# An RWKV scan feeding a SoLU layer: three weight pieces loaded ahead of the second chunk, and one split moved behind the exponential

## The chip, the core and the metric

The kernel runs on one core of a Trainium2 chip. The metric is the device time of one execution in microseconds, median of three runs: 345.81 us (345.55 to 346.35) for the kernel before. The profile is of one execution of its own and counts from the first to the last instruction: 343.4 us.

## The reference

Two parts stand one behind the other. The first is a linear recurrence over time (RWKV) for 4 batches, 8 heads, 768 steps and a head size of 48; its output is read as a matrix `x` of 3072 rows and 384 columns. The second is a SoLU layer on `x`:

```python
for t in range(S):
    cur = einsum('bhd,bhe->bhde', u * kt, vt)
    y[:, :, t] = einsum('bhd,bhde->bhe', rt, state + cur)
    state = w[..., None] * state + einsum('bhd,bhe->bhde', kt, vt)
h = x @ w_in                                # 384 -> 1024
sm = softmax(h);  solu = h * sm
ln = (solu - mean) / sqrt(var + 1e-6) * g_ln
return ln @ w_out                           # 1024 -> 384
```

The weights `w_in` and `w_out` arrive as 64-bit floats, and the kernel turns them into 32-bit floats itself, as integers.

## The kernel before

**Tiling.** The 3072 rows are 24 chunks of 128 rows (6 time steps of the tiling by 4 batches, the batch running fastest, so chunks 0 to 3 are the four batches' first rows). Every chunk goes through two stages: attention, which makes its `xT` (the chunk's `x`, turned), and the layer, which makes its output rows. The layer of a chunk trails its attention.

**Order of the work.** Nothing is planned by a scheduler: under `manual_schedule` every engine executes its instructions in the order in which the Python code issues them, and waits on semaphores for what the other engines have to deliver. So moving one call moves its instructions in the queues of all engines that it uses, and what stands behind a waiting instruction on its engine waits too.

**Steps of a chunk's attention in the prologue** (L1031 to L1105, chunks 0 to 4), by the names that the text uses:

- `load(i, "kr")`, `load(i, "v")` (L472): rows of k, r and v, each 192 KB, issued on SyncE's queue (SP).
- `decay_k(i)` (L697): GpSimd (POOL) multiplies k by a table of decays, tile `kp`.
- `weigh(i)` (L710, L711): POOL makes `rku` = k u r in two multiplications. `sum_own(i)` (L715): VectorE (DVE) sums it per head into `own`. `diagonal(i)` (L729): ScalarE (ACT) writes eight diagonal matrices from `own` into `AT`, the score matrix of the chunk.
- `turn_r(i)` (L741, L742): TensorE (PE) transposes r, DVE multiplies it out of PSUM. `turn_k(i)` (L749, L751): PE transposes `kp`, ACT copies it out.
- `whole_scores(i)` (L764): PE multiplies k and r into the two score banks. `take_scores(i)` (L788): DVE copies them under a mask over `AT`, two instructions. 
- `whole_y(i)` (L815): PE multiplies `AT` and v. `take_y(i)` (L864): ACT copies the result out as `xT`. `whole_outer(i)` (L889) and `update(i)` (L910 to L916): the new state.

**Weights.** `w_in` is cut into six pieces of 512 KB (0 to 5: pieces 0, 1, 2 are the three row blocks of its first 512 columns, 3, 4, 5 those of the other 512), `w_out` into eight of 384 KB (6 to 13). A piece is loaded by `load_weights` (L511) and converted in three steps on three engines: `convert_a` (L522, ACT, the low words), `convert_b` (L535, L537, DVE, the high words), `convert_c` (L545, POOL, their sum). `take_up(p)` is `convert_a(p)` and the load of the next piece that is not yet loaded.

**The layer.** `ffn_in(j)` (L926, L931): six matmuls, three for each half of 512 columns (`ffn_in(0, (0,))` and `(0, (1,))` in the prologue do one half each), then ACT's exponential `e`. There is one `h_ps` buffer, so the next `ffn_in` waits until `unit(j)` has read it: DVE's reciprocal and product (L937, L939), then two passes on ACT (L941, L942). `halve_ln(j)` (L977, ACT) splits the chunk's result into 16-bit halves in a buffer `halves`, from which a transposing DMA (L966) makes another; `join_ln(j)` (L971, DVE) joins them to `lnT`; `ffn_out(j)` (L1016, PE) multiplies with `w_out`. `halve_rk` and `join_rk` do the same for r and k of later chunks. The `halves` buffers and the raw weight pieces are one pool of six.

**Fillers.** `spin(n)` (L593) is n matmuls of the identity into the `h_ps` buffer, of no use but to keep TensorE busy.

**The steady loop** (L1180 to L1260) takes two chunks, a pair, at a time: attention of chunks i and i + 1, `ffn_in` and `unit` of j = i - 2 and j + 1, `ffn_out` of l = i - 7 and l + 1. Its first turn is i = 7, the second pair is i = 9. On ACT the second pair's queue begins, in the kernel before:

```python
if l + 2 < N:
    halve_ln(l + 2)        # ACT: 16-bit halves, needs a free `halves` buffer
for n in first:
    diagonal(n)            # ACT: 8 instructions
join_ln(l + 1)             # DVE
...
if j < N and not late:
    ffn_in(j)              # PE, then ACT: exponential
    unit(j)                # DVE, ACT
```

Of the kernel before, what the change touches and what calls it, by code (L numbers as in the profile page):

```python
# [399 lines left out]
def direct_path(  # L400
# [29 lines left out]
    nc = tc.nc  # L430
# [10 lines left out]
    LA, LO, FIRST, WHOLE = 2, 5, 9, 7  # L441
# [26 lines left out]
    def load(i, which="krv"):  # L468
        b, c = units[i]
        for t, src, n in ((kpads, k, "k"), (rpads, r, "r"), (vts, v, "v")):  # L470
            if n in which:
                nc.sync.dma_start(out=t[i % len(t)][:, :, 0:D],  # L472
                                  in_=src[b, :, ts(c, T), :].rearrange("h s d -> s h d"))
# [34 lines left out]
    def load_weights(j, tag="raw", bufs=6):  # L508
        dst, src, _ = pieces[j]
        raws[j] = wpool.tile([128, dst.shape[1], 2], U32, tag=tag, name="raw", bufs=bufs)  # L510
        nc.sync.dma_start(out=raws[j].rearrange("p n o -> p (n o)"), in_=src)  # L511
# [13 lines left out]
    def convert_b(j):  # L525
        hi, low = step[j]
        n = low.shape[1]
        ma = wpool.tile([128, n], U32, tag="ma", name="ma", bufs=4)
        part = ma
        if pieces[j][2] is None:  # L530
            part = psM.tile([128, n], F32, tag="m", name="part").bitcast(U32)

        nc.vector.tensor_scalar(out=part, in0=hi, scalar1=3, scalar2=0x3FFFFFF8,  # L535
                                op0=ALU.logical_shift_left, op1=ALU.bitwise_and)
        nc.vector.scalar_tensor_tensor(out=ma, in0=hi, scalar=0xC0000000, in1=part,  # L537
                                       op0=ALU.bitwise_and, op1=ALU.bitwise_or)
        step[j] = ma, low

    def convert_c(j):
        dst, _, f = pieces[j]
        ma, low = step[j]

        nc.gpsimd.tensor_tensor(out=dst.bitcast(U32) if f is None else ma, in0=ma, in1=low,  # L545
                                op=ALU.add)
# [19 lines left out]


    load(0, "kr")
    load_weights(0)
    load(1, "kr")  # L570
    load(0, "v")
    load_weights(1)
    load(2, "kr")
    load_weights(2)
    load(1, "v")
    load_weights(3)
    load_weights(4)
    load_weights(5)
    load(3, "kr")
    load(2, "v")  # L580
# [8 lines left out]
    def spin(n):  # L589

        ps = psH.tile([128, dff], F32, tag="h", name="spin")
        for _ in range(n):
            nc.tensor.matmul(ps[:, 0:128], ident, ident, start=True, stop=True)  # L593
# [67 lines left out]
    N = len(units)  # L661
# [32 lines left out]
    def decay_k(i):  # L694
        X = live.setdefault(i, {})
        X["kp"] = apool.tile([128, H, P], F32, name="kp", bufs=5)
        nc.gpsimd.tensor_mul(X["kp"].rearrange("p h d -> p (h d)"),  # L697
                             kpads[i % NLD].rearrange("p h d -> p (h d)"),
                             kdec.rearrange("p a d -> p (a d)"))
# [8 lines left out]
    def weigh(i, engine):  # L708
        rku = live[i]["rku"] = apool.tile([128, H, D], F32, name="rku")
        engine.tensor_mul(rku, kpads[i % NLD][:, :, 0:D], u_bc)  # L710
        engine.tensor_mul(rku, rku, rpads[i % NLD][:, :, 0:D])  # L711

    def sum_own(i):
        own = live[i]["own"] = small.tile([128, H, 1], F32, name="own")
        nc.vector.tensor_reduce(out=own[:, :, 0], in_=live[i]["rku"], axis=AX.X, op=ALU.add)  # L715
# [21 lines left out]
    def turn_r(i):  # L737
        rT = factors(i)["rT"]
        ps = psM.tile([128, HP, T], F32, tag="m", name="tr_ps")
        for a in range(HP):  # L740
            nc.tensor.transpose(ps[:, a, :], pair(rpads[i % NLD], a), ident)  # L741
        nc.vector.tensor_mul(rT, ps, fore)  # L742

    def turn_k(i):
        X = live[i]
        ps = psM.tile([128, HP, T], F32, tag="m", name="tk_ps")

        for a in range(HP):
            nc.tensor.transpose(ps[:, a, :], pair(X["kp"] if i > 0 else kpads[0], a), ident)  # L749
        if i > 0:  # L750
            nc.scalar.copy(out=X["kT"], in_=ps)  # L751
        else:
            nc.vector.tensor_mul(X["kT"], ps, back)
# [30 lines left out]
    def take_scores(i):  # L784
        A4 = live[i]["AT"].rearrange("p (a q) t -> p a q t", q=2)
        mask = later if i < WHOLE else later_half
        for q in range(2):
            nc.vector.copy_predicated(A4[:, :, q, :], mask.to_broadcast([128, HP, mask.shape[2]]),  # L788
                                      live[i]["scores"][q])
# [69 lines left out]
    def take_y(i):  # L859
        X = live[i]  # L860
        X["xT"] = fpool.tile([128, KD, 128], F32, name="xT", bufs=LA + 1)
        n = T // len(X["y"])
        for c, y in enumerate(X["y"]):
            nc.scalar.copy(out=X["xT"][:, :, ts(c, n)], in_=y)  # L864
# [159 lines left out]
    def take_up(p):  # L1024
        nonlocal ahead
        convert_a(p)
        if ahead < len(pieces):
            load_weights(ahead)
            ahead += 1
# [9 lines left out]
    spin(2)  # L1039
    whole_scores(0)  # L1040
    convert_b(0)
    decay_k(1)
    weigh(1, nc.gpsimd)
    turn_r(1)
    spin(4)
    turn_k(1)
    take_scores(0)
    convert_c(0)
    sum_own(1)
    take_up(1)  # L1050
    diagonal(1)
    spin(3)
    whole_y(0)
    whole_outer(0)
    convert_b(1)
    convert_c(1)
    whole_scores(1)
    update(0)
    take_y(0)
    decay_k(2)  # L1060
    weigh(2, nc.gpsimd)
    turn_r(2)
    take_up(2)
    spin(4)
    turn_k(2)
    take_scores(1)
    convert_b(2)
    convert_c(2)
    load(5, "kr")
    load(3, "v")  # L1070
    whole_y(1)
    whole_outer(1)
    whole_scores(2)
    take_up(3)
    take_y(1)
    convert_b(3)
    convert_c(3)
    sum_own(2)
    ffn_in(0, (0,))
    take_up(4)  # L1080
    convert_b(4)
    convert_c(4)
    load(6, "kr")
    load(4, "v")
    take_up(5)
    diagonal(2)
    convert_b(5)
    convert_c(5)
    ffn_in(0, (1,))
    update(1)  # L1090
    take_scores(2)
# [88 lines left out]
    for i in range(LA + LO, N + LA + LO, 2):  # L1180
        j, l = i - LA, i - LA - LO

        late = i == LA + LO
        for n in (i + 5,) if late else (i + 6, i + 7):
            if n < N:
                load(n, "kr")
        for n in (i + 3, i + 4) if not late else ():
            if n < N:
                load(n, "v")
        first, second = ([n] if n < N else [] for n in (i + 2, i + 3))  # L1190
        if late:
            decay(i + 3)
            diagonal(i + 1)
            halve_k(i + 3)
            ffn_in(j)
            attend([i, i + 1])
            halve_r(i + 3)
            unit(j)
            sum_own(i + 3)
            load(i + 3, "v")  # L1200
            load(i + 4, "v")
        decay(i + 4)
        for n in (j - 2, j - 1):
            if LO - 1 <= n < N:
                deviation(n)
        decay(i + 5)
        if l + 2 == N:
            check_sums()
        if l + 2 < N:
            halve_ln(l + 2)  # L1210
        for n in first:
            diagonal(n)
        join_ln(l + 1)
        for n in first:
            join_rk(n)
        if j < N and not late:
            ffn_in(j)
            unit(j)
            within([i, i + 1])
        if i + 4 < N and not late:  # L1220
            halve_rk(i + 4)
        check_next()
        ffn_out(l)
        if late:
            load(i + 6, "kr")
            within([i, i + 1])
            ffn_in(j + 1)
            halve_rk(i + 4)
            load(i + 7, "kr")
        for n in (i, i + 1):  # L1230
            if n < N:
                carried(n)
        if l + 3 < N:
            halve_ln(l + 3)
        for n in (i, i + 1):
            if n < N:
                take_y(n)
        for n in (i, i + 1):
            if n < N:
                update(n)  # L1240
        if late:
            unit(j + 1)
        for n in second:
            join_rk(n)
        if j + 1 < N and not late:
            ffn_in(j + 1)
        for n in second:
            diagonal(n)
        if j + 1 < N and not late:
            unit(j + 1)  # L1250
        ffn_out(l + 1)
        halve_rk(i + 5)
        for n in (i + 4, i + 5):
            if n < N:
                sum_own(n)
        attend([i + 2, i + 3])
        if l + 2 < N:
            join_ln(l + 2)
        if i >= N - 7:
            check_next()  # L1260
# [43 lines left out]
```

## Time and profile before

| | |
|---|---|
| time, median (lowest to highest) | 345.81 us (345.55 to 346.35) |
| span in the profile, granted TensorE clock | 343.4 us, 0.996 |
| `h_ps` matmuls (L926), `o_ps` matmuls (L1016) | 129.9 us, 128.3 us busy |
| ACT copies to `halves` (L977) | 45.3 us busy, 10.2 us idle before them, waiting for a DMA |
| DMA | 52.69 MB, mean 153 GB/s |

The page gives the busy time of each engine, the chain of work that ended last, and groups of instructions with the idle time of their engine just before them. A line of a timeline reads: start, length (us), engine, source line, operation, tiles, number of instructions merged, and in brackets the idle time before the first of them and what ended it. A line of a table of waits reads: who waited for whom, us in total, times, the longest. The chain that ended last is 73% TensorE. From 112 us to the end TensorE's timeline has no gap; the gaps, and the fillers, lie before that.

### The profile page before, as it was taken

How to read it: one execution, taken by the hardware profiler on the slowest of the kernel's cores; microseconds unless marked ns; L12 is line 12 of the kernel's file. 1: busy time of each engine (PE TensorE's matmuls, PEld its weight loads, DVE VectorE, ACT ScalarE, POOL GpSimd, SP SyncE). 2: the span in 40 equal slices, each digit the busy share in tenths (PEclk: the TensorE clock that was granted, in tenths of full speed). 3: DMA queues.
4: the chain of work that ended last, by engine and by line, in shares of the span. 5: the costliest groups of instructions: out<-in, count | busy, mean ns of one | idle time of the engine just before them, and what ended most of it. 6: DMA issues, size and time to landing. Idle time of an engine off the chain costs nothing.

```text
span 343.4 us, 10629 instructions
## 1 busy us (share of the span) xinstructions
PE 332.8 (97%) x4483; PEld 198.9 (58%) x4483; DVE 210.6 (61%) x379; ACT 234.4 (68%) x477; POOL 174.4 (51%) x202
## 2 busy tenths in 40 slices
PE   8989999999998999999999999999999999999993
PEld 6856566655565556556556556555555555555563
DVE  8796988889766487576576577575365052332410
ACT  4776887997945968885784794796594466456510
POOL 7798987699997387682683683630300000000000
PEclk9999999999999999999999999999999999999998
DMA  7999998389999999989969969859841432454541
GB/s 149 243 252 215 253 210 135 68 107 196 208 154 191 174 224 177 205 145 171 198 132 177 212 105 155 186 112 153 191 105 38 122 101 63 99 130 111 131 99 40
DMA packets 164742, 52.69 MB, mean 153 GB/s; under 512 B 157901, under 2 KB 161102, under 8 KB 164686
## 3 DMA queue, kind: packets, MB, share of 16 engines
q1 hardware_dynamic: 164684, 51.92, 80.8%
q8 instruction: 37, 0.61, 0.8%
q14 instruction: 19, 0.16, 0.2%
q10 hardware_dynamic: 2, 0.00, 0.0%
HBM read 26.75 MB, written 4.72 MB: 92 GB/s over the span
## 4 chain that ended last, share of the span: by engine, by line
PE 73%; POOL 11%; ACT 4%; DVE 4%; issue 3%; DMA 2%; SPq 0%; ACTq 0%; POOLq 0%; DVEq 0%
PE o_ps L1016 32%; PE h_ps L926 30%; PE at L854 3%; POOL kp L697 3%; PE at L843 3%; POOL rku L711 2%; POOL rku L710 2%; PE at L781 2%; DMA halves<-halves 2%; POOL rp L704 2%; PE kv_ps L880 1%; ACT AT L729 1%; PE y_ps L815 1%; POOL state L914 1%; DVE ma L537 1%
## 5 line engine op out<-in xcount | busy, mean ns | idle before, releaser
L926 PE MATMUL h_ps<-w_in_sb,xT 128*128 128x512 f32 x288 | 129.9, 600 | 2.0 <-DVE solu L939 2.0
L1016 PE MATMUL o_ps<-w_out_sb,lnT 128*128 128x384 f32 (+1 forms) x400 | 128.3, 476 | 0.0
L1016 PEld LDWEIGHTS o_ps<-w_out_sb,lnT 128*128 128x128 f32 x400 | 74.3, 190 | 48.9 <-issue 4.3
L926 PEld LDWEIGHTS h_ps<-w_in_sb,xT 128*128 128x128 f32 x288 | 52.7, 190 | 61.9 <-issue 57.0
L931 ACT ACTIVATE e<-h_ps 128x1024 f32<-128x1024 f32 x24 | 24.6, 1024 | 40.7 <-PE h_ps L926 40.7
L977 ACT COPY halves<-solu 128x2048 uint16<-128x2048 uint16 x24 | 45.3, 1889 | 10.2 <-DMA halves<-halves 10.2
L914 POOL TENSOR_TENSOR state<-state,pw 48x192 f32<-48x192 f32 x32 | 23.1, 722 | 49.1 <-DVE state L910 47.1
L971 DVE COPY lnT<-halves 128x2048 uint16<-128x2048 uint16 x24 | 39.5, 1660 | 10.7 <-DMA halves<-halves 10.4
L941 ACT ACTIVATE solu<-solu,st 128x1024 f32<-128x1024 f32 x24 | 27.5, 1146 | 24.7 <-DVE solu L939 24.7
L948 POOL TENSOR_SCALAR st<-st 128x1 f32<-128x1 f32 x24 | 4.7, 195 | 64.2 <-ACT e L942 64.1
L710 POOL TENSOR_TENSOR rku<-kpad,u_bc 128x384 f32<-128x384 f32 x24 | 31.9, 1329 | 9.7 <-DVE own L715 8.9
L729 ACT ACTIVATE AT<-same,own 128x64 f32<-128x64 f32 x136 | 34.2, 338 | 0.0
L697 POOL TENSOR_TENSOR kp<-kpad,kdec 128x512 f32<-128x512 f32 x24 | 30.6, 1275 | 3.6 <-ACT kdec L646 1.6
L711 POOL TENSOR_TENSOR rku<-rku,rpad 128x384 f32<-128x384 f32 x24 | 31.3, 1303 | 1.9
L939 DVE SCALAR_TENSOR_TENSOR solu<-h_ps,st,e 128x1024 f32<-128x1024 f32 x24 | 30.8, 1284 | 2.0
L565 DVE TENSOR_REDUCE least<-mag 128x1 f32<-128x384 f32 (+1 forms) x14 | 8.5, 607 | 35.3 <-ACT mag L563 35.3
L937 DVE RECIPROCAL st<-sums 128x1 f32<-128x1 f32 x24 | 3.8, 160 | 40.5 <-ACT e L931 40.0
L1018 ACT ACTIVATE o<-o_ps,st 128x384 f32<-128x384 f32 (+1 forms) x25 | 13.9, 558 | 18.6 <-PE o_ps L1016 12.6
L942 ACT ACTIVATE e<-solu 128x1024 f32<-128x1024 f32 x24 | 25.4, 1057 | 0.8
L971 DVE COPY rk<-halves 128x2048 uint16<-128x2048 uint16 x15 | 25.2, 1679 | 0.2
L788 DVE COPY_PREDICATED AT<-later_half,at 128x256 f32<-128x256 uint32 x34 | 12.5, 438 | 16.1 <-PE at L781 15.7
L704 POOL TENSOR_TENSOR rp<-rpad,rdec 128x512 f32<-128x512 f32 x15 | 21.2, 1414 | 0.0
(105 smaller groups left out, 388.6 us busy)
## 6 DMA issues: line engine op xcount, KB each, us to landing
raw<-in_moe_w_in_dram SPq DMA_DIRECT2D x12, 512.0 KB, 5.2
raw<-in_moe_w_out_dram SPq DMA_DIRECT2D x16, 384.0 KB, 3.8
kpad<-in_k_dram SPq DMA_DIRECT2D x24, 192.0 KB, 4.9
rpad<-in_r_dram SPq DMA_DIRECT2D x24, 192.0 KB, 5.0
vt<-in_v_dram SPq DMA_DIRECT2D x24, 192.0 KB, 5.5
out_dram<-o SPq DMA_DIRECT2D x23, 192.0 KB, 3.4
halves<-halves SPq DMA_TRANSPOSE x39, 5.3
out_dram<-o SPq DMA_DIRECT2D x2, 96.0 KB, 2.7
```

The costliest lines, as they stand in the source:

```text
L697: nc.gpsimd.tensor_mul(X["kp"].rearrange("p h d -> p (h d)"), kpads[i % NLD].rearrange("p h d -> p (h d)"), kdec.rearrange("p a d -> p (a ...
L704: nc.gpsimd.tensor_mul(X["rp"].rearrange("p h d -> p (h d)"), rpads[i % NLD].rearrange("p h d -> p (h d)"), rdec.rearrange("p a d -> p (a ...
L710: engine.tensor_mul(rku, kpads[i % NLD][:, :, 0:D], u_bc)
L711: engine.tensor_mul(rku, rku, rpads[i % NLD][:, :, 0:D])
L729: nc.scalar.activation(out=AT[:, h, :], in_=unit_matrix, func=ACT.Copy, scale=X["own"][:, h])
L914: nc.gpsimd.tensor_mul(S, S, wT)
L926: nc.tensor.matmul(h_ps[:, ts(n, NX)], X["xT"][:, j, :], w_in_sb[:, j, ts(n, NX)], start=(j == 0), stop=(j == KD - 1))
L939: nc.vector.scalar_tensor_tensor(out=solu, in0=X["h"], scalar=rs, in1=X["e"], op0=ALU.mult, op1=ALU.mult, accum_out=tot)
L941: nc.scalar.activation(out=solu, in_=solu, func=ACT.Identity, scale=-float(dff), bias=tot)
L971: nc.vector.tensor_copy(out=words.bitcast(U16).rearrange("p n (t o) -> p o n t", o=2), in_=turned)
L977: nc.scalar.copy(out=both.rearrange("p (o n) -> p o n", o=2), in_=split(X["solu"]))
L1016: nc.tensor.matmul(o_ps, X["lnT"][:, f, :], w_out_sb[:, f, part], start=(f == 0), stop=(f == KF - 1))
```

## The change

It has two parts, and no instruction is added or taken out but four fillers.

The first is a new order of the prologue. In the loads, v of chunk 0 and the pieces 0, 1 and 2 of `w_in` now stand ahead of k and r of chunk 1. The calls behind it are reordered to suit: the conversions of pieces 0 and 1 come before chunk 1's attention, pieces 2 and 3 in the midst of it, `weigh(2)` behind the conversion of piece 4, the first half of `ffn_in(0)` ahead of chunk 2's transposes, and one `spin(4)` (in the kernel before between `turn_r(2)` and `turn_k(2)`) is gone. It is meant to have the first matmuls of the layer ready for TensorE earlier.

The second concerns the second pair alone: `halve_ln(l + 2)` is issued behind `ffn_in(j)` and `unit(j)` instead of ahead of `diagonal`, so that on ACT the exponential no longer stands behind a copy that waits for its buffer.

```diff
     load(0, "kr")
+    load(0, "v")
     load_weights(0)
+    load_weights(1)
+    load_weights(2)
     load(1, "kr")
-    load(0, "v")
-    load_weights(1)
+    load_weights(3)
+    load(1, "v")
+    load_weights(4)
     load(2, "kr")
-    load_weights(2)
-    load(1, "v")
-    load_weights(3)
-    load_weights(4)
     load_weights(5)
...
     whole_scores(0)
     convert_b(0)
+    convert_c(0)
+    take_up(1)
+    convert_b(1)
     decay_k(1)
+    spin(4)
+    take_scores(0)
+    turn_r(1)
+    spin(3)
+    turn_k(1)
     weigh(1, nc.gpsimd)
-    turn_r(1)
-    spin(4)
-    turn_k(1)
-    take_scores(0)
-    convert_c(0)
-    sum_own(1)
-    take_up(1)
-    diagonal(1)
-    spin(3)
     whole_y(0)
     whole_outer(0)
-    convert_b(1)
+    take_up(2)
+    take_y(0)
     convert_c(1)
-    whole_scores(1)
-    update(0)
-    take_y(0)
-    decay_k(2)
-    weigh(2, nc.gpsimd)
-    turn_r(2)
-    take_up(2)
-    spin(4)
-    turn_k(2)
-    take_scores(1)
     convert_b(2)
     convert_c(2)
+    whole_scores(1)
+    sum_own(1)
+    diagonal(1)
+    update(0)
+    take_up(3)
+    convert_b(3)
+    convert_c(3)
+    ffn_in(0, (0,))
+    decay_k(2)
+    turn_r(2)
     load(5, "kr")
     load(3, "v")
+    take_up(4)
+    convert_b(4)
+    take_scores(1)
+    turn_k(2)
+    convert_c(4)
     whole_y(1)
     whole_outer(1)
+    take_y(1)
+    weigh(2, nc.gpsimd)
+    take_up(5)
+    convert_b(5)
+    convert_c(5)
     whole_scores(2)
-    take_up(3)
-    take_y(1)
-    convert_b(3)
-    convert_c(3)
     sum_own(2)
-    ffn_in(0, (0,))
-    take_up(4)
-    convert_b(4)
-    convert_c(4)
...
-    take_up(5)
     diagonal(2)
-    convert_b(5)
-    convert_c(5)
     ffn_in(0, (1,))
     update(1)
     take_scores(2)
...
-        if l + 2 < N:
+
+        second_pair = i == LA + LO + 2
+        if l + 2 < N and not second_pair:
             halve_ln(l + 2)
...
             unit(j)
             within([i, i + 1])
+        if second_pair:
+            halve_ln(l + 2)
```

## The prediction, made blind

> **What bounds the kernel now.** I read the page's busy times first, then who TensorE (PE) waited for, then timelines. The page:
>
> ```profile
> PE 332.8 (97%) x4483; PEld 198.9 (58%) x4483; DVE 210.6 (61%) x379; ACT 234.4 (68%) x477; POOL 174.4 (51%) x202
> ```
>
> The waits of PE over the whole span:
>
> ```profile
> PE h_ps L926 <- DVE solu L939: 2.0, 2, 1.6
> PE tk_ps L749 <- POOL kp L697: 1.7, 2, 1.5
> ```
>
> PE is busy for 332.8 of 343.4 us. The change takes away no useful matmul, so it can win only PE's idle time and fillers, or add to them. One wait is in the prologue, the larger part of the other (1.6 of 2.0) at the second pair. PE's timeline of the prologue:
>
> ```profile
> 16.59 1.06 PE L593 MATMUL spin<-ident 128*128 128x128 f32 x8
> 19.10 0.66 PE L749 MATMUL tk_ps<-ident,kp 128*128 128x128 f32 x4 [1.46 <-POOL kp L697]
> ...
> 22.06 5.49 PE L926 MATMUL h_ps<-w_in_sb,xT 128*128 128x512 f32 x12
> 27.48 1.08 PE L815 MATMUL y_ps<-AT,vt 128*32 128x128 f32 x32
> ```
>
> Filler and wait from 16.59 to 19.10 are 2.5 us without use. The last line is `whole_y(2)`, which starts at 27.48 without a wait. Ahead of it PE has done the scores of chunks 0 to 2, `whole_y` of 0 and 1 and all of `ffn_in(0)`. The changed kernel has exactly this set ahead of `whole_y(2)`, and the same instructions behind. Its start is therefore my yardstick for the prologue.
>
> What delivers to it, from the timelines of ACT and DVE (chunk 0's `AT`, the first `low`, chunk 0's `take_scores`), then of POOL:
>
> ```profile
> 9.71 2.45 ACT L729 ACTIVATE AT<-ident,own 128x128 f32<-128x128 f32 x8
> 12.06 0.66 ACT L522 ACTIVATE low<-raw 128x512 uint32<-128x512 uint32 x1
> ...
> 12.01 1.35 DVE L788 COPY_PREDICATED AT<-later,at 128x512 f32<-128x512 uint32 x2
> ```
>
> ```profile
> 9.89 2.52 POOL L697 TENSOR_TENSOR kp<-kpad,kdec 128x512 f32<-128x512 f32 x2 [1.60 <-ACT kdec L646]
> ...
> 19.00 1.01 POOL L710 TENSOR_TENSOR rku<-kpad,u_bc 128x384 f32<-128x384 f32 x1
> 20.09 1.02 POOL L711 TENSOR_TENSOR rku<-rku,rpad 128x384 f32<-128x384 f32 x1
> 21.08 2.52 POOL L545 TENSOR_TENSOR w_in_sb<-ma,low 128x512 uint32<-128x512 uint32 x2
> 23.77 2.60 POOL L545 TENSOR_TENSOR w_in_sb<-ma,low 128x512 uint32<-128x512 uint32 x2 [0.17 <-DVE ma L537]
> ```
>
> The reader is to see that `weigh(2)` (19.00 to 21.1) stands ahead of four conversions. So `AT` of chunk 2 is made early (ACT, 23.28), and `take_scores(2)` (25.61 to 26.96) is over before PE wants it. The second pair, on ACT, DVE and PE:
>
> ```profile
> 105.15 1.90 ACT L977 COPY halves<-solu 128x2048 uint16<-128x2048 uint16 x1 [6.97 <-DMA halves<-halves]
> 106.95 2.02 ACT L729 ACTIVATE AT<-same,own 128x64 f32<-128x64 f32 x8
> 108.88 1.00 ACT L931 ACTIVATE e<-h_ps 128x1024 f32<-128x1024 f32 x1
> ...
> 105.15 1.69 DVE L971 COPY lnT<-halves 128x2048 uint16<-128x2048 uint16 x1 [4.37 <-DMA halves<-halves]
> 106.73 2.15 DVE L971 COPY rk<-halves 128x2048 uint16<-128x2048 uint16 x1
> 110.00 0.16 DVE L937 RECIPROCAL st<-sums 128x1 f32<-128x1 f32 x1 [1.13 <-ACT e L931]
> 110.27 1.29 DVE L939 SCALAR_TENSOR_TENSOR solu<-h_ps,st,e 128x1024 f32<-128x1024 f32 x1
> ...
> 111.62 5.42 PE L926 MATMUL h_ps<-w_in_sb,xT 128*128 128x512 f32 x12 [1.55 <-DVE solu L939]
> ```
>
> **What the Trainium skill says.** "TensorE: Matmul & The Clock Gate", section "Architectural detail", has ACT, DVE and GpSimd as strict FIFO queues; the trace agrees, with ACT idle for 6.97 us before the split although the exponential's input was ready at 101.8. The same page, section "What's actually happening", has PE fall to half its clock after an idle window of about 3.4 us; before's longest gap in the prologue is 1.46 us, so it doesn't show this. "DMA: Bandwidth & Descriptors", section "Queues, rings and completion order", has each engine take a ring's descriptors in order; the trace agrees: chunk 1's k and r, issued at 3.80 and 4.28 behind piece 0 (issued 3.07), land 5.7 and 6.2 us later, at 9.5 and 10.5, behind that piece (8.2).
>
> **The prologue, step by step.** The loads: in the stretch from 4.0 to 22.6 us DMA moved 261 GB/s without a gap, so a later place is a later landing. Pieces 1 and 2 and v of chunk 0 (512, 512, 192 KB) now come ahead of k and r of chunk 1: 1.25 MB at 261 GB/s is 4.8 us, less where large pieces go faster, so r lands at 14 to 15.3 instead of 10.5. I take 14.4. PE ends its spins at about 11.8 and waits for it.
>
> The second chain needs no late load. Durations are those of the lines above, POOL's from start to start (1.25 a multiplication or conversion of 512, 2.05 a `weigh`):
> ACT writes `AT` of chunk 0 and then `low` of piece 0, as before, until 12.72.
> POOL: `convert_c(0)`, now ahead of chunk 1's `kp`, 12.75 to 14.0; `kp` to 15.25; `weigh(1)` to 17.3 (before: 14.4).
> DVE: `sum_own(1)`, 0.55, to 17.85. ACT: `diagonal(1)`, 2.4, to 20.25; only behind it, in its queue, `low` of piece 3, 0.65, to 20.9.
> POOL, which has done pieces 1 and 2 by 19.8 and waits: `convert_c(3)` to 22.15, `decay_k(2)` to 23.4, `convert_c(4)` to 24.65, and only then `weigh(2)`, to 26.7 (before: 21.1).
> DVE: `sum_own(2)` to 27.2. ACT: `diagonal(2)` from 27.2. For chunk 0 the scores were in `AT` 3.65 us after its start (9.71 to 13.36), so here at 30.9, and `whole_y(2)` can't start in earnest before.
>
> That is 30.9 - 27.48 = 3.4 us late, the lower end. Two additions: `convert_c(4)` also needs `convert_b(4)`, queued on DVE behind chunk 2's r, which PE transposes only behind the first half of `ffn_in(0)`, and this hangs on r of chunk 1 and on DVE's 1.4 us for the conversion. With r at 14.4 it costs 0.4, with 15.3 about 0.9. I take 3.8, with 3.4 and 4.3 as ends. The spin removed gives nothing back, since PE waits there anyway (for `kp` of chunk 2 until 23.4 or later, then for `take_scores(1)`). The remaining moves (`take_y`, `update`, the fourth `w_out` load ahead of chunk 5's k) lie in those waits or beside PE's 4 us of lateness and cost nothing. Behind `whole_y(2)` PE's timeline is dense to 41.2, so nothing is won back there; at 41.68 it waited 0.47 for DVE, whose queue may be freer then: I take -0.2 (0 to -0.47).
>
> **The second pair.** Without the split ahead of them, ACT does `diagonal` from about 98.2 and the exponential at 101.8. What then holds DVE's reciprocal is its own queue: the joins wait for the same DMA (105.15) and end at 108.88. The product then starts at 108.9 + 0.27 = 109.17 instead of 110.27, PE 1.35 behind it as before: 110.5 instead of 111.62. Saved: 1.1 (no more than 1.55). The split's 1.9 us now lie on ACT behind the two passes of `unit`, from about 112.6. ACT reaches the next exponential at about 119.5, the product ends at about 122.2, and PE wants the `h_ps` buffer at 123.96 - 1.1 = 122.9: hidden, with 0.7 to spare. Its transpose was issued at 113.31 and now from 114.5; `lnT` was joined at 126.70 and used at 130.72: hidden.
>
> Sum: 3.8 - 0.2 - 1.1 = +2.5, so 345.8 + 2.5 = 348.3.
>
> **The rivals.** (1) Faster: DVE and ACT keep ahead, and `whole_y(2)` doesn't wait for `weigh(2)`. PE then loses the 2.5 us of filler and wait, pays about 2.3 for r of chunk 1 (11.8 to 14.1), and gains 1.1 and up to 0.5 at the other places: 344. The durations on POOL speak against it; only much shorter ones would do. (2) No change: late by 3.4, of which 1.55 and 0.47 come back, and some more in small gaps: 345.8 to 346.5. (3) The second pair's gain is lost to the next wait (the 0.7 to spare is used up, or the DMA chain is what counts): 345.8 + 3.8 - 0.2 = 349.4. (4) PE's wait for chunk 1's r outlasts the clock's window, and the prologue's matmuls run at half speed: about 2 us more, 350.5.
>
> **How the numbers follow.** 348.3 at 0.66; (3) at 0.14; (4) at 0.07; (2) at 0.06; (1) at 0.07. Slower 0.88, within 0.2% 0.05, faster 0.07. Ends of the main case: 3.4 - 0.47 - 1.55 = +1.4 and 4.3 - 0.9 = +3.4, so 347.2 to 349.2; with (3) and a share of the disturbed cases on both sides, 346.4 to 350.2.
>
> **What would show it.** Right: `whole_y(2)` starts at 30.9 to 31.8; `weigh(2)` ends at 26.5 to 27.8; PE shows waits for r or `kp` of chunks 1 and 2 and for `AT`; no idle time of 7 us before the split on ACT, and under 0.6 on PE at the second pair. Wrong: `whole_y(2)` before 29, or a wait later on, at the third pair, that takes the second pair's gain.

## The result, and the profile after

The changed kernel takes 350.58 us (median of 4 runs, 349.66 to 351.3). The kernel before, run beside it on the same chip, takes 345.68 us. The ratio is 1.0137, with a 95% interval of 1.0108 to 1.0166: the change makes the kernel 4.9 us slower. The forecast of slower was right, but 2.5 us was too little, and the time lies just above the upper end of the range.

First, as before, the busy times of the page after:

```profile
PE 334.3 (96%) x4475; PEld 199.6 (57%) x4475; DVE 208.5 (60%) x379; ACT 234.3 (67%) x477; POOL 175.0 (50%) x202
```

TensorE (PE) was busy 1.5 us *longer*, although four fillers are gone. So besides new waits, some of its work got slower. The waits of PE after, over the whole span (who waited for whom, us in total, times, longest):

```profile
PE tr_ps L741 <- DMA rpad<-in_r_dram: 3.3, 2, 3.1
PE y_ps L815 <- DVE AT L788: 1.8, 4, 0.8
PE tk_ps L749 <- POOL kp L697: 1.3, 1, 1.3
PE h_ps L926 <- DVE solu L939: 1.2, 1, 1.2
```

Two names are new: r of chunk 1 from the DMA, and the score matrices `AT`. The old waits, for `kp` and for the second pair's product, have shrunk a little and not gone. PE's timeline of the prologue after:

```profile
15.09 0.63 PE L741 MATMUL tr_ps<-ident,rpad 128*128 128x128 f32 x4 [3.07 <-DMA rpad<-in_r_dram]
...
17.28 1.94 PE L815 MATMUL y_ps<-AT,vt 128*32 128x128 f32 x32
...
23.40 0.60 PE L741 MATMUL tr_ps<-ident,rpad 128*128 128x128 f32 x4
25.30 0.66 PE L749 MATMUL tk_ps<-ident,kp 128*128 128x128 f32 x4 [1.29 <-POOL kp L697]
26.75 0.41 PE L815 MATMUL y_ps<-AT,vt 128*32 128x128 f32 x4 [0.79 <-DVE AT L788]
...
33.13 0.41 PE L815 MATMUL y_ps<-AT,vt 128*32 128x128 f32 x4 [0.57 <-DVE AT L788]
33.74 0.96 PE L815 MATMUL y_ps<-AT,vt 128*32 128x128 f32 x26 [0.20 <-DVE AT L788]
...
35.08 0.66 PE L741 MATMUL tr_ps<-ident,rpad 128*128 128x128 f32 x4
```

The yardstick, `whole_y(2)`, gets going at 33.74 rather than 27.48, 6.3 us late. The prediction had 31.3. The second line is `whole_y(0)`: its 32 matmuls take 1.94 us, where the same 32 in `whole_y(2)` took 1.08 in the kernel before. The busy times by stretch show why. One row each for 10 to 20 us (busy us and instructions of PE, PEld, DVE, ACT and POOL, then the granted clock, the DMA share and GB/s), first of before, then of after:

```profile
10.00:20.00 10.00, 8.33 (x176) 7.25 (x170) 8.15 (x15) 7.50 (x22) 9.11 (x8) 1.00 1.04 272
```

```profile
10.00:20.00 10.00, 6.93 (x133) 6.07 (x132) 6.62 (x11) 5.43 (x16) 8.14 (x7) 0.83 1.11 266
```

The granted clock fell to 0.83 over this stretch. Taken by single microseconds it is 1.00 up to 16 us, 0.57, 0.50, 0.50 and 0.72 from 16 to 20, and 1.00 after that. It fell behind the 3.07 us in which PE waited for r. That is the prediction's rival (4), which had a chance of 0.07.

The prediction's chain that delivers `whole_y(2)` is on POOL and ACT. POOL's timeline after (conversions of pieces 0, 3 and 4 are the lines of L545, `weigh(2)` the last two), then ACT's (the copy of `take_y(0)`, `diagonal(1)`, `diagonal(2)`):

```profile
13.05 1.28 POOL L545 TENSOR_TENSOR w_in_sb<-ma,low 128x512 uint32<-128x512 uint32 x1 [1.62 <-DVE ma L537]
...
22.73 1.28 POOL L545 TENSOR_TENSOR w_in_sb<-ma,low 128x512 uint32<-128x512 uint32 x1 [2.64 <-ACT low L522]
...
26.20 1.27 POOL L545 TENSOR_TENSOR w_in_sb<-ma,low 128x512 uint32<-128x512 uint32 x1 [0.96 <-DVE ma L537]
27.43 1.01 POOL L710 TENSOR_TENSOR rku<-kpad,u_bc 128x384 f32<-128x384 f32 x1
28.52 1.01 POOL L711 TENSOR_TENSOR rku<-rku,rpad 128x384 f32<-128x384 f32 x1
...
19.28 0.48 ACT L864 COPY xT<-y_ps 128x384 f32<-128x384 f32 x1 [0.73 <-PE y_ps L815]
19.66 2.45 ACT L729 ACTIVATE AT<-ident,own 128x128 f32<-128x128 f32 x8
...
30.15 2.45 ACT L729 ACTIVATE AT<-ident,own 128x128 f32<-128x128 f32 x8 [0.60 <-DVE own L715]
```

These lines can be laid beside the prediction's chain, step by step (us; the predicted column has its 0.4 in it from piece 4 on):

| step | predicted | after | late by |
|---|---|---|---|
| `convert_c(0)` starts, POOL | 12.75 | 13.05 | 0.3 |
| `weigh(1)` ends, POOL | 17.3 | 17.6 | 0.3 |
| `diagonal(1)` starts, ACT | 17.85 | 19.66 | 1.8 |
| `convert_c(3)` starts, POOL | 20.9 | 22.73 | 1.8 |
| `convert_c(4)` starts, POOL | 23.8 | 26.20 | 2.4 |
| `weigh(2)` ends, POOL | 27.1 | 29.53 | 2.4 |
| `diagonal(2)` starts, ACT | 27.6 | 30.15 | 2.5 |
| `whole_y(2)`, PE | 31.3 | 33.74 | 2.4 |

Every link is there, in the predicted order, but up to `convert_c(3)` the chain is not what held `whole_y(2)`. POOL was free at 25.24 and waited another 0.96 us, for `convert_b(4)` on DVE. This is the input of `convert_c(4)` that hangs on r of chunk 1, and for which the prediction added 0.4. The chain of the work that ended last, followed back from `whole_y(2)`, runs through it (start, length, what; "issue" is time without a wait that the profile shows):

```profile
6.64 8.31 DMA rpad<-in_r_dram
14.95 0.14 issue
15.09 0.63 PE tr_ps L741 x4
...
20.79 2.77 PE h_ps L926 x6
23.57 0.45 PE tr_ps L741 x4
...
24.04 0.69 DVE rk L742
...
25.37 0.70 DVE ma L537
...
26.20 0.04 POOL w_in_sb L545
```

From chunk 1's transpose (15.09) to the first half of `ffn_in(0)` (20.72) PE took 5.63 us. The kernel called "both moves" below has the same matmuls between them and starts at the same moment, at a clock of 1.00:

```profile
15.16 0.60 PE L741 MATMUL tr_ps<-ident,rpad 128*128 128x128 f32 x4
...
19.16 2.84 PE L926 MATMUL h_ps<-w_in_sb,xT 128*128 128x512 f32 x6
```

There it takes 4.00 us, so the low clock costs 1.6 us on this path. The rest of the path, 2.68 us from that half to chunk 2's transpose (23.40) and 2.80 on to `convert_c(4)`, gives back the prediction's number: with its r at 14.4, 14.4 + 4.00 + 2.68 + 2.80 is 23.9, beside its 23.8. So its 0.4 had these matmuls at the full clock. Of the 2.4 us at `convert_c(4)`, then, 0.7 come from r (15.09 rather than 14.4) and 1.6 from the clock.

The delay of 1.8 us at `diagonal(1)` lies beside this path. The kernel of both moves starts `diagonal(1)` at 18.44, so 1.2 of the 1.8 are the clock's here too: `whole_y(0)` at half speed is what `take_y(0)` waits for (0.73), and `take_y(0)` stands ahead of `diagonal(1)` on ACT.

Behind the prologue PE is 6.25 us late at chunk 3's transpose, 35.08 against 28.83. The line of the kernel before:

```profile
28.83 0.66 PE L741 MATMUL tr_ps<-ident,rpad 128*128 128x128 f32 x4
```

At the second `ffn_in` behind the prologue it is 5.5 late, since the wait of 0.47 at 41.68 is gone. The second pair after, on ACT, DVE and PE:

```profile
107.41 1.03 ACT L931 ACTIVATE e<-h_ps 128x1024 f32<-128x1024 f32 x1 [1.83 <-PE h_ps L926]
...
110.77 2.42 DVE L971 COPY lnT<-halves 128x2048 uint16<-128x2048 uint16 x1 [4.70 <-DMA halves<-halves]
113.09 2.15 DVE L971 COPY rk<-halves 128x2048 uint16<-128x2048 uint16 x1
115.14 0.14 DVE L937 RECIPROCAL st<-sums 128x1 f32<-128x1 f32 x1
...
116.73 5.42 PE L926 MATMUL h_ps<-w_in_sb,xT 128*128 128x512 f32 x12 [1.17 <-DVE solu L939]
```

The exponential runs as soon as its input is there, and the reciprocal stands behind the two joins alone, as predicted. But the joins take 4.37 us (110.77 to 115.14) rather than 3.73, and PE still waits 1.17. So PE's lateness falls only from 5.5 to 5.1 here, and 5.2 remain at the last block of matmuls (332.67 against 327.45).

### The profile page after: what moved, and what is told of

Its sections match the earlier page's. It is cut to its first block, busy times and chain, and to the rows that moved or that the text cites. A ratio compares the mean times of both kernels' runs of the same rounds, so it can differ in the third digit from the quotient of the medians.

```text
span 349.2 us, 10612 instructions
## 1 busy us (share of the span) xinstructions
PE 334.3 (96%) x4475; PEld 199.6 (57%) x4475; DVE 208.5 (60%) x379; ACT 234.3 (67%) x477; POOL 175.0 (50%) x202
## 4 chain that ended last, share of the span: by engine, by line
PE 88%; DMA 4%; DVE 3%; SPq 1%; issue 1%; ACT 1%; POOL 1%; DVEq 0%; POOLq 0%
PE h_ps L926 35%; PE o_ps L1016 35%; PE at L854 3%; PE at L843 3%; PE at L781 3%; PE y_ps L815 3%; DMA rpad<-in_r_dram 2%; PE kv_ps L880 2%; DMA halves<-halves 2%; PE at L764 1%; PE tr_ps L741 1%; PE tk_ps L749 1%; DVE lnT L971 1%; PE kv_ps L889 1%; SPq L511 1%
## 5 line engine op out<-in xcount | busy, mean ns | idle before, releaser
L948 POOL TENSOR_SCALAR st<-st 128x1 f32<-128x1 f32 x24 | 5.9, 244 | 64.2 <-ACT e L942 64.1
L710 POOL TENSOR_TENSOR rku<-kpad,u_bc 128x384 f32<-128x384 f32 x24 | 31.7, 1322 | 8.4 <-DVE own L715 7.6
L704 POOL TENSOR_TENSOR rp<-rpad,rdec 128x512 f32<-128x512 f32 x15 | 22.7, 1514 | 0.4 <-DMA rpad<-in_r_dram 0.4
```

## The experiments

The questions: is the second pair's term right, and where does it go? Is it the loads or the calls that cost the prologue its time? How much is the clock's? And which queue holds `whole_y(2)`?

**The second pair alone, and the prologue alone.** The first kernel is the one before with the move of `halve_ln` and nothing else. The second is the changed kernel with that move taken back.

```diff
+        second_pair = i == LA + LO + 2
-        if l + 2 < N:
+        if l + 2 < N and not second_pair:
             halve_ln(l + 2)
...
+        if second_pair:
+            halve_ln(l + 2)
```

> The kernel before with only the second pair's split moved behind the exponential. My theory: the changed kernel lost at the prologue, and this part alone is a small gain, 0.4 to 1.1 us (the wait of TensorE for h_ps at the second pair falls from 1.55 us to 0.4 to 1.2, as in the changed kernel, and the wait of 0.47 near 41.7 us stays): 344.6 to 345.3 us. Rival: the later split costs as much at the third pair as it wins, no change: 345.7.

> The changed kernel with the split back in its old place: the new prologue alone. My theory: all of the loss, and the small gain of the second pair missing: 350.9 to 351.7 us, whole_y(2) at 33 to 34 us as in the changed kernel. Rival: the split's move is part of the loss, then this is faster than the changed kernel, below 350.4.

Measured: the move alone gives 344.73 us, a ratio of 0.9966 (0.9949 to 0.9982). The prologue alone gives 352.43, 1.0199 (1.0158 to 1.024). The second pair of the move alone, on DVE and PE:

```profile
105.07 1.62 DVE L971 COPY lnT<-halves 128x2048 uint16<-128x2048 uint16 x1 [4.43 <-DMA halves<-halves]
...
110.19 5.42 PE L926 MATMUL h_ps<-w_in_sb,xT 128*128 128x512 f32 x12 [0.31 <-DVE solu L939]
```

And of the prologue alone, on ACT, DVE and PE:

```profile
111.86 1.90 ACT L977 COPY halves<-solu 128x2048 uint16<-128x2048 uint16 x1 [7.73 <-DMA halves<-halves]
...
111.86 2.16 DVE L971 COPY lnT<-halves 128x2048 uint16<-128x2048 uint16 x1 [4.98 <-DMA halves<-halves]
...
118.33 5.42 PE L926 MATMUL h_ps<-w_in_sb,xT 128*128 128x512 f32 x12 [2.29 <-DVE solu L939]
```

In both settings the move is worth what was worked out: 1.55 - 0.31 = 1.24 us without the new prologue, 2.29 - 1.17 = 1.12 with it. The second pair's wait would have grown from 1.55 to 2.29 without the move, because the new prologue sends it to the second pair in another phase. That is why the wait went down by only 0.38 from before to after. The whole loss, and more, is in the prologue: about 6.5 us in time, 6.9 in the spans (350.3 against 343.4). The prologue alone took longer than was expected of it. Its chunk 3 comes 0.4 us later than the changed kernel's (35.50 against 35.08), and its clock was at 0.91 and 0.92 from 20 to 40 us as well.

**The loads alone, and the calls alone.** The first has the changed order of loads under the calls of before, with the split where it was; its diff against the kernel before is shown. The second has all of the change except the order of the loads.

```diff
     load(0, "kr")
-    load_weights(0)
-    load(1, "kr")
     load(0, "v")
+    load_weights(0)
     load_weights(1)
-    load(2, "kr")
     load_weights(2)
-    load(1, "v")
+    load(1, "kr")
     load_weights(3)
+    load(1, "v")
     load_weights(4)
+    load(2, "kr")
     load_weights(5)
```

> The kernel before with the loads in the changed order, and nothing else of the change. Theory that the late landing of chunk 1's k and r (14.1 and 15.0 us rather than 9.5 and 10.5) is a cost of its own under the old calls, because POOL multiplies k and weighs chunk 1 ahead of all conversions: weigh(1) ends near 17.5 rather than 14.4, everything behind it on POOL comes 3 us later, whole_y(2) starts near 30.5 rather than 27.5, and the time is 348.5 to 350. Rival that the loads are hidden and the order of the calls is the whole cost: 345.5 to 346.5, whole_y(2) before 28.5.

> The changed kernel with the loads in the order of before (r of chunk 1 lands near 10.5 us again, piece 2 of w_in near 17.3), the calls of the engines in the new order. Theory of the prediction: POOL's order, with weigh(2) behind five conversions, holds whole_y(2) at 30.5 to 31.5 us whatever the loads do: 347.8 to 348.8 us. Rival: the late landing of chunk 1's rows is the whole cause, then whole_y(2) is at 28 us or earlier and the time is 344.5 to 346.

Measured: the loads alone 350.76 us, 1.0133 (1.0081 to 1.0185). The calls with the old loads 350.05, 1.0122 (1.0083 to 1.0162), with the second pair's 1.1 or 1.2 us already in it as a gain. Each half alone costs about 5 us and the two together 6.5: they are not added up, as each makes chunk 1 late in its own way. PE's timeline, for the loads alone:

```profile
15.04 1.08 PE L741 MATMUL tr_ps<-ident,rpad 128*128 128x128 f32 x4 [4.21 <-DMA rpad<-in_r_dram]
```

And for the calls alone:

```profile
15.36 0.66 PE L749 MATMUL tk_ps<-ident,kp 128*128 128x128 f32 x4 [2.43 <-POOL kp L697]
15.95 1.91 PE L815 MATMUL y_ps<-AT,vt 128*32 128x128 f32 x32
```

With the new loads PE waits for chunk 1's r. With the old loads r is there in time, but the calls put `convert_c(0)` ahead of chunk 1's `kp` on POOL, and PE waits for `kp` to about the same moment. In both, the matmuls behind the wait take about twice as long, and the granted clock of the stretch from 10 to 20 us is 0.66 and 0.83. So the expectation that loads are hidden is refuted, and so is the reading that they are the whole cause: either order suffices. Both kernels came out slower than their theories had them. The theories left out the clock, which falls in both.

**The clock.** The changed kernel with sixteen fillers in place of four ahead of chunk 1's transpose, so that PE is busy until r has landed:

```diff
     decay_k(1)
-    spin(4)
+    spin(16)
     take_scores(0)
     turn_r(1)
```

> The changed kernel with 16 spins instead of 4 ahead of turn_r(1), so that TensorE works through its wait for chunk 1's r. Theory of the clock: the 3.1 us wait lets the granted clock fall (0.83 in the stretch from 10 to 20 us), the matmuls of chunk 1 take twice as long, and as POOL, ACT and DVE hang on them, whole_y(2) comes 1.5 to 2 us earlier here: 348.6 to 349.1 us. Rival, that TensorE's slow matmuls are hidden behind POOL's queue: within 0.4 us of the changed kernel.

Measured: 348.95 us, 1.0092 (1.0062 to 1.0121), 1.6 us less than the changed kernel, whose interval (1.0108 to 1.0166) it just overlaps. In the traces `whole_y(2)` comes 1.1 us earlier and chunk 3's transpose 0.7; another 0.5 lies at the second pair (a wait of 0.68 instead of 1.17), where no filler stands. PE's wait for r shrank to 0.25 us, `whole_y(0)` took 1.08, and the clock was 1.00 from 10 to 20 us. But it then fell to 0.83 in the stretch from 20 to 30. On ACT, POOL and PE:

```profile
17.92 2.45 ACT L729 ACTIVATE AT<-ident,own 128x128 f32<-128x128 f32 x8 [0.25 <-DVE own L715]
...
21.00 1.27 POOL L545 TENSOR_TENSOR w_in_sb<-ma,low 128x512 uint32<-128x512 uint32 x1 [1.22 <-ACT low L522]
...
25.33 1.28 POOL L545 TENSOR_TENSOR w_in_sb<-ma,low 128x512 uint32<-128x512 uint32 x1 [1.83 <-DVE ma L537]
...
22.51 0.63 PE L741 MATMUL tr_ps<-ident,rpad 128*128 128x128 f32 x4 [1.31 <-DMA rpad<-in_r_dram]
...
25.88 2.33 PE L815 MATMUL y_ps<-AT,vt 128*32 128x128 f32 x30 [1.67 <-DVE AT L788]
...
32.67 1.29 PE L815 MATMUL y_ps<-AT,vt 128*32 128x128 f32 x30
```

With PE at its full clock ("warm"), `diagonal(1)` starts at 17.92 and `convert_c(3)` at 21.00: the prediction had 17.85 and 20.9. (Chunk 1's transpose also starts 0.8 us earlier in this trace, at 14.32.) Then a second link shows. `convert_c(4)` waits 1.83 us on POOL for `convert_b(4)`. That stands on DVE behind r of chunk 2, and PE can't transpose this r before it lands (1.31 of wait). With the old order of the loads r of chunk 2 lands at 14.9 to 15.1 us (four traces; that of the kernel before doesn't show it). Behind pieces 3 and 4 it lands at 22.4 here and at 22.7 in the changed kernel, which didn't wait for it, because its PE was later still (23.40). The prediction never dated it.

**Which queue holds whole_y(2).** From the warm kernel, three kernels: `take_scores(1)` moved ahead of chunk 2's r on DVE; `decay_k(2)` and `weigh(2)` moved ahead of the conversion of piece 3 on POOL, with `sum_own(2)` ahead of `convert_b(5)`; and both moves.

```diff
     convert_c(2)
+    decay_k(2)                # second move
+    weigh(2, nc.gpsimd)       # second move
     whole_scores(1)
...
     ffn_in(0, (0,))
-    decay_k(2)                # second move
+    take_scores(1)            # first move
     turn_r(2)
...
     convert_b(4)
-    take_scores(1)            # first move
+    sum_own(2)                # second move
     turn_k(2)
...
-    weigh(2, nc.gpsimd)       # second move
...
-    sum_own(2)                # second move
```

> The kernel of run warm with take_scores(1) ahead of turn_r(2), so that on VectorE it no longer stands behind chunk 2's r and behind convert_b(4). If VectorE's queue alone is what holds the prologue once TensorE is kept warm, all the rest of the loss goes: 346 us or less. My theory is that two queues hold it in turn: whole_y(1) starts 1.5 us earlier, at 24 to 24.5 us, but weigh(2) still ends at 28 to 28.7 us on POOL behind convert_c(4), and whole_y(2) comes at 32 us or later: 347.8 to 348.8 us.

> The kernel of run warm with decay_k(2) and weigh(2) ahead of convert_c(3) on POOL and sum_own(2) ahead of convert_b(5) on VectorE. If POOL's order alone is the cause, as the prediction had it, whole_y(2) comes at 30 us or earlier and the time is below 347. My theory of two queues: weigh(2) ends near 23.7 us instead of 28.6, but TensorE arrives at whole_y(2) no earlier, since whole_y(1) still waits for take_scores(1) until 25.9 us: 348.4 to 349.2 us, as run warm.

> Both moves at once, on the kernel of run warm; the loads stay in the changed order. Theory of two queues that hold the prologue in turn: now whole_y(2) starts at 29 to 30 us, 3 to 4 us earlier than in run warm, and the time falls to 345.6 to 346.8 us. Rival, that the late landing of chunk 1's and 2's rows is what is left: no better than the better of the two single moves, 348 us or more.

| kernel | time (us) | ratio (95% interval) | `whole_y(1)`, PE's wait for it | `whole_y(2)`, PE's wait | chunk 3's transpose |
|---|---|---|---|---|---|
| warm | 348.95 | 1.0092 (1.0062 to 1.0121) | 25.88, 1.67 | 32.67, none | 34.35 |
| first move | 348.74 | 1.0078 (1.0049 to 1.0107) | 24.84, none | 32.10, 1.38 | 33.44 |
| second move | 348.53 | 1.0074 (1.0050 to 1.0099) | 25.55, 2.51 | 32.28, none | 33.64 |
| both | 346.20 | 1.0010 (0.9977 to 1.0043) | 22.81, none | 29.04, none | 30.39 |

Neither move alone brings anything that the intervals tell from the warm kernel; both together bring 2.7 us. (With the second move alone the clock falls again, to 0.83 from 20 to 30 us as in the warm kernel; in the other two it stays at 1.00. In the warm kernel the slow matmuls come only behind the start of `whole_y(1)`, and there the kernel with both is 3.1 us ahead already, 22.81 against 25.88. So most of the gain is not the clock's.) With the first alone, PE gets through `whole_y(1)` and stands at `whole_y(2)` for the `AT` of the late `weigh(2)`. With the second alone, it stands at `whole_y(1)` for the mask copy behind chunk 2's r. The two queues hold PE to almost the same moment, one after the other. PE's timeline of the kernel with both:

```profile
22.81 1.08 PE L815 MATMUL y_ps<-AT,vt 128*32 128x128 f32 x32
...
29.04 1.08 PE L815 MATMUL y_ps<-AT,vt 128*32 128x128 f32 x32
```

It still has the changed order of the loads. With the queues' order mended and PE kept busy, chunk 3's transpose is 1.6 us later than in the kernel before (28.83), and the time 1.5 us above that of the split alone (344.73). That is what is left of the prologue's 6.5.

**The clock, with the queues mended.** The last kernel with four fillers again in place of sixteen:

```diff
-    spin(16)
+    spin(4)
```

> The changed kernel with the two moves of the queues (take_scores(1) ahead of chunk 2's r on DVE; decay_k(2) and weigh(2) ahead of the conversion of piece 3 on POOL), but with the four fillers ahead of chunk 1's r as in the change, so that TensorE waits about 3 us for r. Theory that the fall of the clock is a cost of its own, apart from the order of the queues: the granted clock shows 0.83 between 10 and 20 us again, whole_y(0) takes about 1.9 us rather than 1.08, and the kernel is 1.0 to 2.0 us slower than with sixteen fillers (346.2), 347.2 to 348.2. Rival that the clock only matters where the queues are late already: within 0.5 us of 346.2.

Measured: median 347.79 us, ratio 1.0033 (1.0015 to 1.0052); the quotient of the medians would be larger, 1.0057. The interval overlaps that of the kernel with sixteen fillers. In the trace the clock is at 0.83 from 10 to 20 us again and `whole_y(0)` takes 1.94, yet chunk 3's transpose starts at 30.88, only 0.5 later than with the warm clock. So the theory's number for the time came in, but the interval and the 0.5 in the trace don't exclude the rival. Its last block of matmuls starts 1.4 us later (330.05 against 328.67), and 0.85 of that lies at the second pair, where PE waits 1.45 instead of 0.60. What the clock alone costs here stays between about 0.5 and 1.6 us. Beside the changed kernel, on the other hand, this run shows that the two moves bring 2.8 us with the clock as low as there, and these intervals lie apart.

**The late r of chunk 2.** From the warm kernel, its load moved ahead of piece 3:

```diff
+    load(2, "kr")
     load_weights(3)
     load(1, "v")
     load_weights(4)
-    load(2, "kr")
     load_weights(5)
```

> The changed kernel with sixteen fillers ahead of chunk 1's r, and k and r of chunk 2 loaded ahead of piece 3. Theory that the late landing of chunk 2's r (22.4 us; 15.0 in the kernel before), which the prediction never dated, is the second floor under the chain: it lands near 17, TensorE's wait for it (1.31 us) goes, chunk 2's transpose starts near 21.2 rather than 22.5, the conversion of piece 4 on POOL near 24.0 rather than 25.3, and whole_y(2) and the time move by 0.9 to 1.4 us, to 347.5 to 348.1 from 348.95. Rival that another link stands at the same place (piece 3, which lands later now, or the chain through AT of chunk 1): 348.5 to 349.5.

Measured: 348.59 us, 1.0085 (1.0056 to 1.0114): no difference that the intervals show. The mechanism did what was expected: r lands at 16.6, PE doesn't wait for it, and `convert_c(4)` waits less. POOL's timeline, and PE's:

```profile
24.64 1.28 POOL L545 TENSOR_TENSOR w_in_sb<-ma,low 128x512 uint32<-128x512 uint32 x1 [0.61 <-DVE ma L537]
...
24.08 0.66 PE L749 MATMUL tk_ps<-ident,kp 128*128 128x128 f32 x4 [1.64 <-POOL kp L697]
```

But now PE waits 1.64 us for `kp` of chunk 2, which stands on POOL behind the conversion of piece 3. `whole_y(2)` moves from 32.67 to 32.19 only, half of the least that was expected. The late landing is one of several things at the same place, and taking it away uncovers the next.

**Can both kernels be beaten?** The kernel before with the split moved, and `decay_k(2)` ahead of `convert_b(1)`; then also `take_scores(1)` ahead of chunk 2's r.

```diff
     whole_outer(0)
+    decay_k(2)
     convert_b(1)
...
     take_y(0)
-    decay_k(2)
     weigh(2, nc.gpsimd)
+    take_scores(1)            # second kernel only
     turn_r(2)
...
-    take_scores(1)            # second kernel only
```

> A version for both kernels to be beaten by: the kernel of run s_only with decay_k(2) ahead of convert_b(1) and convert_c(1), so that POOL makes chunk 2's kp at about 15.7 us, in an idle time of 0.8 us, and not at 17.8. TensorE's wait before chunk 2's transposed k (0.9 to 1.5 us) goes; whole_y(1) then waits for take_scores(1), which ends at 19.0 us, so whole_y(2) gains 0.5 to 0.9 us: 343.6 to 344.4 us. Rival, that the gain is taken by w_in's pieces, which POOL converts behind it: 344.7, as s_only.

> The kernel before with the split moved behind the exponential, decay_k(2) ahead of the conversion of piece 1, and take_scores(1) ahead of chunk 2's r on DVE. Theory that whole_y(1) waits for the mask copy in DVE's queue: TensorE's wait of 0.37 us ahead of whole_y(1) goes, and the time is 343.9 to 344.4. Rival that the first half of ffn_in(0) then waits for its weights instead (0.65 and 0.20 us with decay_k(2) early): no change from 344.5 within 0.2.

Measured: 344.53 us, 0.9963 (0.9947 to 0.9979), and 345.58, 0.9983 (0.9966 to 1.0001). The first takes PE's wait for `kp` away but is not to be told from the split alone (0.9966). In its place stand waits of 0.65 and 0.20 for the weights of `ffn_in(0)`, as the rival said. The second starts chunk 3's transpose 0.7 us earlier, but its time isn't better. Its profile shows PE's wait at the second pair at 1.28 instead of 0.30, and the `lnT` join at 2.26 instead of 1.33; the last section comes back to this. So the split behind the exponential by itself is the version to keep; `decay_k(2)` adds nothing that the runs show. It is 1.2 us faster than the kernel before and 6 faster than the changed one.

## Why the prediction was right in direction and short in size

- **The yardstick and the order of the queues: right.** `whole_y(2)` does stand behind `convert_c(4)` and `weigh(2)`, and the links ahead of them are 0.3 to 1.8 us late. That queues hold it, the runs show from the other side: with two moves in the queues 2.7 us come back at the full clock, and 2.8 at the low one.
- **`convert_c(4)` behind r of chunk 1, priced at 0.4 (0.9 with r at 15.3): this step failed.** The path was the right one, r of chunk 1, PE's matmuls to the first half of `ffn_in(0)`, chunk 2's r, `convert_b(4)`; its price holds only if PE does these matmuls at the full clock. They took 5.63 us and not 4.00. With r 0.7 later than assumed, this path became the one that held `whole_y(2)`: `convert_c(4)` at 26.20 rather than 23.8, which is all of the 2.4 that the prologue lost beyond the forecast.
- **Rival (4), the clock: left out of the sum, and too low at 0.07.** Its condition was a wait that outlasts the clock's window. The Trainium skill's "TensorE: Matmul & The Clock Gate", section "What's actually happening", gives this window as about 3.4 us, and the prediction's own wait was 2.6 (11.8 to 14.4). The wait that came was 3.07, still shorter than the window, and the clock fell all the same. It also fell behind single waits of 2.19 and 2.43 us, so by these runs a forecast wait of 2.6 was no reason to put the clock at nothing. Its price of 2 us was near the 1.6 of the path. That its 350.5 is so close to 350.58 is in part luck, since two other terms were off and nearly cancel.
- **"The remaining moves (`take_y`, `update`, ...) ... cost nothing": wrong for `diagonal(1)`, without effect on the time as far as the trace shows.** `take_y(0)` now stands ahead of `diagonal(1)` on ACT and waits for `whole_y(0)` on PE, so the chain that "needs no late load" hangs on one after all, and `diagonal(1)` started at 19.66 and not at 17.85. But `convert_c(4)` waited longer for the other input. No run moved `take_y(0)` alone.
- **r of chunk 2: not dated.** It lands at 22.7 us with the new order. In the changed kernel PE comes later than that; once the clock is kept up, this landing is the next thing that holds, and so the sixteen fillers brought less at `whole_y(2)` (1.1) than the 1.6 of the path.
- **r of chunk 1 at 14.4: right within its ends.** It landed at 14.95.
- **-0.2 at 41.68: right in kind, short in size.** The wait of 0.47 is gone, and some 0.3 in small gaps with it: 0.8 in all, where 0.47 was the most that was forecast.
- **The second pair, -1.1: right as the move's own worth** (1.24 and 1.12), but the pair itself lost 0.7 through the new prologue, so that "under 0.6 on PE" came out as 1.17. Rival (3) forecast this loss, through the DMA chain or a next wait. It was neither: the two joins took 4.37 us rather than 3.73. The next `h_ps` buffer is in time, as the single wait in the table of waits shows.

The sum by the trace: +6.3 at `whole_y(2)`, -0.8 up to the second `ffn_in` behind the prologue, -0.4 at the second pair, +5.1, against a measured 4.9. The prediction had +3.8 - 0.2 - 1.1 = +2.5. So nearly all of the miss is the prologue's 2.4, and the other two differences nearly cancel.

## What to carry to other kernels

When a prediction has TensorE waiting, price what TensorE does behind the wait as well: here a wait of 3 us was followed by matmuls at half speed, which cost another 1.6 us on the path. When a step needs two inputs, carry both of their times through to the end, for the one that was behind can become the later. Date every transfer that the new order of loads delays, not only the one that the change talks about. And when several queues hold an engine to about the same moment, mending one of them shows nothing: here two moves gave nothing apart and 2.7 us together.

## What the runs showed of the hardware

**The clock can fall behind short waits.** Matmuls of 128 rows take twice as long behind a wait of 2.43 us (1.91 for 32 of them, where 1.08 is usual), and the transpose behind one of 2.19 us takes 1.09 instead of 0.60. In the kernel with sixteen fillers three waits of 1.31, 0.41 and 1.67 us within 5 us were followed by a `whole_y(1)` of 2.33 us. So a sum of short waits seems to do it too. But like waits did not always do it: 1.29, 0.79 and 0.20 us in the changed kernel from 24 to 28 us, and a single 1.89 in the kernel with the first move, left the clock at 1.00 (20 to 30 us), while 1.02, 1.07 and 0.20 with the calls alone were followed by 0.83. No threshold comes out of these runs.

**A 16-bit copy on VectorE stands still while a GpSimd multiplication runs.** The `lnT` join of the second pair took 1.32 to 2.44 us in fourteen traces, always for 128 x 2048 elements. An undisturbed join takes 1.32. Beside it, GpSimd multiplies `rp` (L704, 1.26 us):

| kernel | overlap with L704 (us) | join (us) | join less overlap |
|---|---|---|---|
| `decay_k(2)` early | 0.15 | 1.33 | 1.18 |
| split alone | 0.43 | 1.62 | 1.19 |
| before | 0.49 | 1.69 | 1.20 |
| both moves, warm | 0.92 | 2.10 | 1.18 |
| prologue alone | 0.97 | 2.16 | 1.19 |
| warm | 1.09 | 2.26 | 1.17 |
| after | 1.25 | 2.42 | 1.17 |

In 13 of 14 traces the last column is 1.17 to 1.20. In the same 13, GpSimd's next multiplication (L710), which starts while the join runs, takes 2.04 to 2.06 us, where 1.01 is usual in the prologue. The one exception is the kernel with the first move alone, where the join starts first. There it takes its plain 1.32, and the multiplication takes 2.38 instead of 1.26. On DVE and POOL:

```profile
108.32 1.32 DVE L971 COPY lnT<-halves 128x2048 uint16<-128x2048 uint16 x1 [3.57 <-DMA halves<-halves]
...
108.35 2.38 POOL L704 TENSOR_TENSOR rp<-rpad,rdec 128x512 f32<-128x512 f32 x1
```

In these traces whoever starts first runs, and the other waits to its end. The Trainium skill's "SBUF — State Buffer", section "Who interferes with whom", describes this as a port pair that VectorE and GpSimd share under an exclusive lock, and the traces agree. What it means here is that the second pair's wait depends on whether the DMA lands before, in or after GpSimd's multiplication: up to 1.1 us, in a place that the change doesn't touch. It accounts for the 0.86 us by which PE's wait in the changed kernel (1.17) exceeds that of the split alone (0.31): its joins take 4.37 us instead of 3.52. It is read from the traces side by side; no run moved the multiplication by itself.
